# One store for the rows shared by four batches, and a new order of a planned kernel

## The chip, the cores and the metric

The kernel runs on one core of a Trainium2 chip. The metric is the device time of one execution in microseconds; the median of several runs is compared. A core has TensorE (PE, with its weight loads PEld), VectorE (DVE), ScalarE (ACT), GpSimd (POOL) and SyncE (SP), each with its own queue of instructions in order, and 16 DMA engines, which move what SP and ACT issue.

## What is computed

The reference chains three layers, all in 32-bit floats. Attention has 4 batches, 8 heads, 512 local and 32 shared (global) rows of width 64. A local row sees its own neighbourhood of 32 to either side and the shared rows, a shared row sees everything. The output is 4 x 544 = 2,176 rows of 512.

```python
out_g = np.matmul(sm(s_g), v_all)
a_l = sm(np.concatenate([s_lg, np.where(mask, s_ll, -1e9)], axis=-1))
out_l = np.matmul(a_l, np.concatenate([v_g, v_l], axis=2))
```

The second layer is dense: `h = x @ w_in` (512 to 1,024), `h * softmax(h)`, a layer norm, `@ w_out` (back to 512). The third is a soft mixture of 8 experts with 4 slots each: `logits = x @ phi`, a softmax over the rows gathers 32 slot inputs, each expert applies `relu(s @ w1) @ w2`, and a softmax over the slots spreads the 32 results over all rows: `out = c @ slot_out`.

## The kernel before, in words

The work is cut into operations, small groups of instructions of one engine with the buffers that they read and write: 1,571 of them. There are 16 tiles of 128 local rows for attention (`local_tile`) and one of shared rows per batch (`global_tile`); 17 dense tiles of 128 rows (`dense_tile`), of which the last, tile 16, holds the 4 x 32 shared rows; and a tail that needs all rows, since the gathering softmax runs over them: expert layers, and the product `c @ slot_out` with its stores (`tail`).

In the trace PE's lines are these. L743 and L821: scores of local and shared rows. L773, L852, L963: transposes on PE (products with the unit matrix L773 and L963 among them). L788 and L863: weights times v. L900: the dense product, 24 per tile, written as three products of rounded parts. L984: logits. L1050: gathering of slots. L1178 and L1225: the two expert layers. L1259: the last product. L883: transposes into a spare buffer that only keep PE active. ACT has the exponentials (L756, L920), many evictions of accumulators (L775, L968, L1265), DVE the maxima, products and the other evictions (L751, L915, L923, L1267).

The last product is done in two pieces of columns, 320 and 192 (`PIECES`), each behind its own half of L1225. Per piece the 16 local tiles are evicted to SBUF in groups of two (320 columns) or four (192) and stored by SP (L1272): 8 stores of 320 KB and 4 of 384 KB. Tile 16 goes separately: its rows 32b to 32b+31 belong to the first 32 rows of batch b, 544 rows apart in the output. `store` (L1269) issues one transfer of 32 rows per batch (L1274), on SP for the first piece and on ACT's queue for the second.

All of the order comes from a planner in the kernel's own text. `Schedule.run` (L170) plays the operations through on a model of the engines, with a duration for each, a latency between each two engines and a pool of 47 SBUF slots (`NSLOT`) and 8 accumulator banks. At each point an idle engine takes, of its operations that are ready and find a buffer, the one with the least number in the table `PRIORITY` (L403; L1344 overwrites the priority that the builder gave). `CAPS` limits how many slots a class of buffers may hold at once (L229), `KEEP` reserves slots for a class that still needs them (L240). On PE an operation whose array shape differs from the one before is handicapped by `STAY` (L259). The durations are arguments of `op`; those of the stores count SP as occupied for the time of the transfer. The engines then get their instructions in the planned order, and on the chip each runs them in order, waiting on semaphores.

SP also issues all loads in its planned order (L554): q, k and v of the batches, the weights of the dense layer (split into high and low parts by DVE, ACT and POOL, L607 to L618) and the 64 blocks of expert weights. A load waits in SP's queue until its slot is free, and what is behind it waits too.

Of the kernel before, what the change touches and what calls it, by code (L numbers as in the profile page):

```python
# [18 lines left out]
B, H, SL, SG, HD = 4, 8, 512, 32, 64  # L19
DM, DF, NE, SPE = 512, 1024, 8, 4  # L20
NS = NE * SPE
SEQ = SL + SG
# [344 lines left out]
def rank(names, name):  # L367
# [6 lines left out]
CAPS = dict(h=12, p1=61, E=13, W=58, eT=24, lT=5, ln=26, q=34, u=14, v=52, wst=13, xhl=67, xp=16)  # L374
KEEP = dict(p1=3, E=2, W=5, eT=2, eg=21, lT=1, ln=3, mkx=10, u=2, v=2, w=8, wo=28, wst=8, xhl=4, xp=1)
# [13 lines left out]
STAY = 0.448683864814  # L389
# [121 lines left out]
def kernel_body(ctx: ExitStack, tc: tile.TileContext, q, k, v, w_in, w_out, phi, gl, w1, w2, cst, out):  # L511
    nc = tc.nc
    ctx.enter_context(tc.manual_schedule())
    sch = Schedule({"sb": NSLOT, "ps": 8}, CAPS, KEEP, {"k": (3, B)})
    buf, slot, op = sch.buf, sch.slot, sch.op
# [609 lines left out]
    def tail():  # L1125
# [17 lines left out]
        for n, (d0, d1) in enumerate(STEPS):  # L1143
            w = 128 * (d1 - d0)
# [294 lines left out]
```

## Time and profile before

| what | us |
|---|---|
| median of 3 runs | 293.09 |
| the three runs | 291.93, 293.09, 294.32 |
| the profiled execution | 293.87 |
| span of the profiled execution, first to last instruction | 292.1 |

The profile's page is taken from one execution. Its span is shorter than that execution's time by 1.8 us, which lie before the first and behind the last instruction. Busy times of PE are modelled from the issue of the matmuls, since these are pipelined.

### The profile page before, as it was taken

The numbers are of one execution on the slowest core, as the hardware profiler recorded it, in microseconds if no ns is written. First come the engines' busy times: TensorE is split into PE (matmuls) and PEld (weight loads), VectorE is DVE, ScalarE is ACT, GpSimd is POOL, SyncE is SP. The second block draws the span as 40 slices with busy tenths as digits, with TensorE's granted clock in tenths as the row PEclk, the third lists the DMA queues.
The fourth block names the chain that finished last, engine by engine and source line by source line (L and its number), as shares of the span: only waits on it lengthen the run. The fifth ranks groups of instructions, "written<-read, shape, count | busy, mean of one in ns | idle before, by whom it ended". The sixth has DMA issues, their size and how long they took to land.

```text
span 292.1 us, 10948 instructions
## 1 busy us (share of the span) xinstructions
PE 265.6 (91%) x4378; PEld 198.9 (68%) x4378; DVE 202.3 (69%) x752; ACT 196.5 (67%) x650; POOL 100.5 (34%) x171
## 2 busy tenths in 40 slices
PE   0268899999999999999999999999999999999992
PEld 0255578877767787787887887868887775354571
DVE  1789999999855599959987989359849851020351
ACT  2499989975979789998689885547556850220331
POOL 2796874822302346132322335034232431300000
PEclk9999799999999999999999999999999999999999
DMA  7999999926955402364792759997587898999297
GB/s 252 378 402 411 407 404 399 369 85 233 305 207 148 156 14 74 122 242 149 249 301 105 218 166 292 352 360 287 145 287 264 328 331 247 301 332 326 74 344 235
DMA packets 33651, 75.23 MB, mean 258 GB/s; under 512 B 3008, under 2 KB 15936, under 8 KB 33216
## 3 DMA queue, kind: packets, MB, share of 16 engines
q1 hardware_dynamic: 33408, 74.43, 73.1%
q8 instruction: 34, 0.56, 0.8%
q14 instruction: 17, 0.14, 0.1%
q10 hardware_dynamic: 192, 0.10, 0.1%
HBM read 67.83 MB, written 4.46 MB: 247 GB/s over the span
## 4 chain that ended last, share of the span: by engine, by line
PE 81%; DMA 6%; DVE 4%; ACT 3%; issue 2%; SPq 0%; ACTq 0%
PE h L900 32%; PE p L743 6%; PE p L1225 5%; PE p L1178 5%; PE p L773 4%; PE p L788 4%; PE p L963 4%; DMA q<-in_q 3%; PE p L984 3%; PE p L1050 2%; PE p L863 2%; DMA mkx<-in_cst 2%; PE p L1259 2%; PE p L852 2%; PE p L883 1%
## 5 line engine op out<-in xcount | busy, mean ns | idle before, releaser
L900 PE MATMUL h<-w,xhl 128*128 128x512 f32 x408 | 106.8, 405 | 1.5 <-issue 0.7
L900 PEld LDWEIGHTS h<-w,xhl 128*128 128x128 f32 x408 | 72.7, 189 | 18.3 <-issue 2.5
L756 ACT ACTIVATE E<-E,nmx 128x128 f32<-128x128 f32 x128 | 49.7, 394 | 1.0 <-DVE nmx L751 0.7
L743 PE MATMUL p<-k,q 64*32 64x128 f32 x1024 | 21.8, 300 | 16.0 <-DMA q<-in_q 15.1
L751 DVE CUSTOM_DVE_ANT_0 E<-p,mkx 128x128 f32<-128x128 f32 x128 | 29.0, 285 | 4.3 <-PE p L743 4.3
L743 PEld LDWEIGHTS p<-k,q 64*32 64x32 f32 x1024 | 16.5, 115 | 20.9 <-issue 15.4
L920 ACT ACTIVATE u<-h,st 128x512 f32<-128x512 f32 x34 | 23.1, 684 | 8.3 <-DVE st L916 8.0
L892 POOL TENSOR_TENSOR xhl<-xp,xhl 128x512 fp32r<-128x512 f32 x16 | 20.6, 1288 | 14.8 <-ACT xhl L891 14.6
L756 ACT ACTIVATION_READ_ACCUMULATOR E<-E,nmx 128x1 f32 x128 | 24.7, 193 | 0.0
L923 DVE SCALAR_TENSOR_TENSOR u<-h,u 128x512 f32<-128x512 f32 x34 | 22.8, 683 | 2.1 <-ACT u L920 2.0
L915 DVE TENSOR_REDUCE st<-h 128x1 f32<-128x512 f32 x34 | 22.6, 685 | 1.3 <-PE h L900 1.3
L773 PE MATMUL p<-cs,E 128*128 128x128 f32 x128 | 20.4, 293 | 1.9 <-ACT w L630 1.2
L974 POOL TENSOR_TENSOR st<-st,eps 128x1 f32<-128x1 f32 x17 | 10.0, 586 | 31.8 <-DVE st L971 31.8
L775 ACT ACTIVATE eT<-p 128x512 f32<-128x512 f32 x32 | 18.2, 593 | 4.0 <-PE p L773 3.7
L969 ACT ACTIVATE u<-ln 128x1024 f32<-128x1024 f32 x17 | 18.1, 1063 | 3.2 <-DVE ln L942 3.2
L788 PE MATMUL p<-v,eT 128*32 128x64 f32 x1024 | 18.9, 222 | 0.3 <-ACT lT L968 0.2
L773 PEld LDWEIGHTS p<-cs,E 128*128 128x128 f32 x128 | 15.7, 148 | 5.1 <-issue 2.0
L788 PEld LDWEIGHTS p<-v,eT 128*32 128x32 f32 x1024 | 16.2, 111 | 3.3 <-issue 0.9
L795 DVE TENSOR_TENSOR eT<-p,r 128x256 f32<-128x256 f32 x32 | 12.7, 418 | 5.3 <-ACT E L756 1.8
L968 ACT ACTIVATE lT<-p 128x512 f32<-128x512 f32 x25 | 14.2, 595 | 2.6 <-PE p L963 2.5
L963 PE MATMUL p<-cs,ln 128*128 128x128 f32 x104 | 15.2, 277 | 0.4 <-DVE eT L795 0.4
L618 POOL TENSOR_SCALAR W<-W 128x512 f32<-128x512 f32 x8 | 11.9, 1492 | 9.4 <-ACT W L617 9.4
(144 smaller groups left out, 533.2 us busy)
## 6 DMA issues: line engine op xcount, KB each, us to landing
unit<-in_w SPq DMA_DIRECT2D x48, 512.0 KB, 5.6
v<-in_v SPq DMA_DIRECT2D x28, 512.0 KB, 6.9
k<-in_k SPq DMA_DIRECT2D x3, 1536.0 KB, 6.4
wst<-in_w_in SPq DMA_DIRECT2D x8, 512.0 KB, 8.9
wst<-in_w_out SPq DMA_DIRECT2D x8, 512.0 KB, 10.6
k<-in_w SPq DMA_DIRECT2D x8, 512.0 KB, 5.2
q<-in_q SPq DMA_DIRECT2D x6, 512.0 KB, 7.6
out<-unit SPq DMA_DIRECT2D x8, 320.0 KB, 4.8
```

Of the source, the lines that this page charges most:

```text
L743: nc.tensor.matmul(out=sp[hh][32 * c : 32 * c + 32, a2 + i, :], lhsT=Q[rows, 4 * (a2 + i) + c, :], rhs=K[rows, c, s : s + 128], start=True ...
L751: nc.vector.tensor_tensor_reduce(out=E[:, hh, a, :], in0=sp[hh][:, a, :], in1=MK(mask_kind(4 * t + a)), scale=-SCALE, scalar=3.0e38, op0=A ...
L756: nc.scalar.activation(out=E[:, hh, a, :], in_=E[:, hh, a, :], func=AF.Exp, bias=nmx[:, hh, a : a + 1], scale=-1.0, accum_out=sm[:, hh, a ...
L773: nc.tensor.transpose(out=tp[:, a, :], in_=E[:, hh, a, :], identity=I())
L775: op("ACT", 478, lambda hh=hh, tp=tp: nc.scalar.activation(out=eT[hh].ap, in_=tp.ap, func=AF.Copy), (tp,), (eT[hh],))
L788: nc.tensor.matmul(out=av[32 * c : 32 * c + 32, hh, a, :], lhsT=eT[hh][:, a, 32 * c : 32 * c + 32], rhs=V[:, (g - 1) % 2, 64 * h : 64 * h ...
L892: op("Pool", 1250, lambda: nc.gpsimd.tensor_tensor(out=xl.ap, in0=X.ap, in1=xh.ap.bitcast(F32), op=ALU.subtract), (X, xh), (xl,), port=True)
L900: nc.tensor.matmul(out=hp[n].ap, lhsT=lhs[:, kt, :], rhs=rhs[kt][n].ap, start=(kt == 0 and lhs is xh and rhs is whi), stop=(kt == 3 and lh ...
L915: op("DVE", 602, lambda n=n: nc.vector.tensor_reduce(out=part(7 + n), in_=hp[n].ap, axis=AX.X, op=ALU.max, negate=True), (hp[n],), (col[7 ...
L920: op("ACT", 664, lambda n=n: nc.scalar.activation(out=u[:, n, :], in_=hp[n].ap, func=AF.Exp, bias=nm(), scale=1.0, accum_out=part(7 + n)), ...
L923: op("DVE", 613, lambda n=n: nc.vector.scalar_tensor_tensor(out=u[:, n, :], in0=hp[n].ap, scalar=1.0, in1=u[:, n, :], op0=ALU.mult, op1=AL ...
L963: nc.tensor.transpose(out=tp[:, n, :], in_=ln[:, f // 2, 128 * (f % 2) : 128 * (f % 2) + 128], identity=I())
```

## The change

The four transfers of tile 16 per piece become one, whose target takes the first 32 rows of each batch and whose source is the whole tile of 128 rows. The prices of full stores in the planner change, and the limits, the reserves, STAY and all numbers of the table are new. The table has 1,565 numbers in place of 1,571.

```diff
-CAPS = dict(h=12, p1=61, E=13, W=58, eT=24, lT=5, ln=26, q=34, u=14, v=52, wst=13, xhl=67, xp=16)
-KEEP = dict(p1=3, E=2, W=5, eT=2, eg=21, lT=1, ln=3, mkx=10, u=2, v=2, w=8, wo=28, wst=8, xhl=4, xp=1)
+CAPS = dict(h=10, p1=67, E=20, W=52, eT=32, lT=8, ln=35, q=40, u=20, v=53, wst=20, xhl=72, xp=20)
+KEEP = dict(p1=1, E=2, W=2, eT=2, eg=16, lT=1, ln=3, mkx=8, q=1, u=2, v=2, w=6, wo=5, wst=5, xhl=4, xp=1)
...
-STAY = 0.448683864814
+STAY = 1.13106627204
...
-                def store(eng, b=None, j0=j0, ob=ob, cols=cols, group=group):
-                    if b is None:
+                def store(eng, rest=False, j0=j0, ob=ob, cols=cols, group=group):
+                    if not rest:
                         r0 = (j0 // 4) * SEQ + SG + 128 * (j0 % 4)
                         eng.dma_start(out=out[r0 : r0 + 128 * group, cols].rearrange("(k p) d -> p k d", p=128), in_=ob.ap)
                     else:
-                        eng.dma_start(out=out[b * SEQ : b * SEQ + SG, cols], in_=ob[32 * b : 32 * b + 32, 0, :])
+                        eng.dma_start(out=out.rearrange("(b s) d -> b s d", b=B)[:, 0:SG, cols], in_=ob[:, 0, :])
                 if j0 < 16:
-                    op("SP", max((1.45 * w + 25.0) * group, 430), lambda store=store: store(nc.sync), obr, ())
+                    op("SP", max((1.28 * w + 52.0) * group, 430), lambda store=store: store(nc.sync), obr, ())
+                elif ends:
+                    op("ACT", 450, lambda store=store: store(nc.scalar, True), obr, ())
                 else:
-
-                    for b in range(B):
-                        if ends:
-                            op("ACT", 450, lambda store=store, b=b: store(nc.scalar, b), obr, ())
-                        else:
-                            op("SP", 430, lambda store=store, b=b: store(nc.sync, b), obr, ())
+                    op("SP", 430, lambda store=store: store(nc.sync, True), obr, ())
```

The table is left out of the diff: every number differs, and a single one says nothing. What the prediction uses of it are the numbers of the PE operations, sorted by size, and of the first loads.

## Rows read from the trace of the kernel before

**Rows 1.** The page, busy time, share of the span and instructions per engine.

```profile
PE 265.6 (91%) x4378; PEld 198.9 (68%) x4378; DVE 202.3 (69%) x752; ACT 196.5 (67%) x650; POOL 100.5 (34%) x171
```

**Rows 2.** Stages: us, then busy of PE, PEld, DVE, ACT, POOL, clock, DMA share, GB/s.

```profile
17.00:36.00 19.00, 16.20 (x358) 12.28 (x359) 17.45 (x73) 18.00 (x65) 14.93 (x15) 0.91 1.03 407
36.00:273.00 237.00, 233.86 (x3782) 175.37 (x3784) 169.25 (x642) 164.88 (x555) 75.86 (x146) 1.00 0.71 242
273.00:287.00 14.00, 13.57 (x183) 9.73 (x175) 6.43 (x15) 6.03 (x15) 0.00 (x0) 1.00 0.71 240
287.00:292.10 5.10, 0.00 (x0) 0.00 (x0) 0.00 (x0) 0.00 (x0) 0.00 (x0) 0.91 0.69 219
```

**Rows 3.** Waits of PE from 36 to 287: us in total, times, longest.

```profile
PE p L743 <- issue: 0.9, 2, 0.7
...
PE p L963 <- DVE eT L795: 0.4, 1, 0.4
```

**Rows 4.** The page, the chain that ended last, by engine.

```profile
PE 81%; DMA 6%; DVE 4%; ACT 3%; issue 2%; SPq 0%; ACTq 0%
```

**Rows 5.** The chain of waits from 207 to 223: start us, us, what.

```profile
209.33 1.38 PE h L900 x6
210.70 0.57 PE p L984 x16
...
211.71 0.44 PE p L984 x16
212.14 1.59 PE h L900 x6
```

**Rows 6.** PE's timeline, 36 to 287, first and last of 383: start us, us.

```profile
35.80 0.86 PE L900 MATMUL h<-w,xhl 128*128 128x512 f32 x3
...
285.58 0.98 PE L883 MATMUL p<-cs 128*128 128x128 f32 x7
```

**Rows 7.** SP's timeline at the end: stores of shared rows, then full stores.

```profile
274.44 1.76 SPq L1274 DMA_DIRECT2D out<-unit  x4
276.31 11.27 SPq L1272 DMA_DIRECT2D out<-unit  x12
```

**Rows 8.** ACT's timeline, 283.5 to 287.1: evictions, and issues on ACT's queue.

```profile
284.32 0.38 ACTq L1274 DMA_DIRECT2D out<-unit  x1
284.81 0.49 ACT L1265 ACTIVATE unit<-p 128x384 f32<-128x384 f32 x1 [0.52 <-ACT unit L1265]
284.83 0.40 ACTq L1274 DMA_DIRECT2D out<-unit  x1
285.28 0.49 ACT L1265 ACTIVATE unit<-p 128x384 f32<-128x384 f32 x1
285.31 1.16 ACTq L1274 DMA_DIRECT2D out<-unit  x2
286.51 0.49 ACT L1265 ACTIVATE unit<-p 128x384 f32<-128x384 f32 x1 [0.73 <-issue]
```

**Rows 9.** SP's timeline from 287 us: the last store.

```profile
287.02 0.55 SPq L1272 DMA_DIRECT2D out<-unit  x1
```

**Rows 10.** Stages of the end, columns as in rows 2.

```profile
284.50:285.50 1.00, 1.00 (x17) 0.97 (x16) 0.57 (x2) 0.69 (x2) 0.00 (x0) 1.00 0.49 155
285.50:290.50 5.00, 1.07 (x11) 0.75 (x7) 0.79 (x2) 0.76 (x2) 0.00 (x0) 1.00 1.01 319
290.50:292.10 1.60, 0.00 (x0) 0.00 (x0) 0.00 (x0) 0.00 (x0) 0.00 (x0) 0.72 0.02 5
```

**Rows 11.** DMA issues: queue, count, KB each, median us to landing.

```profile
out<-unit SPq DMA_DIRECT2D x4, 384.0 KB, 3.7
...
out<-unit SPq DMA_DIRECT2D x4, 40.0 KB, 1.6
```

**Rows 12.** The v blocks' loads, 60 to 200 us.

```profile
DMA to landing us min/median/max: 3.5/5.5/8.5
```

**Rows 13.** Waits of SP's queue, 60 to 180: us in total, times, longest.

```profile
SPq L554 <- DVE xp L799: 14.8, 3, 11.7
```

**Rows 14.** The chain of waits at 134 us: start us, us, what.

```profile
134.14 3.36 DMA v<-in_v
```

205 rows, old and new, of the table PRIORITY are left out of this document.

## The prediction, made before the changed kernel ran

> **What bounds the kernel now.** I read the busy shares first [rows 1]: PE 91% of the 292.1 us span, DVE and ACT under 70%. That is an average, so the stages come next [rows 2]. Between 36 and 273 us PE is busy 233.86 of 237.00 us at a granted clock of 1.00; before that (17 to 36) 2.8 us of 19 are open, and in the last stage PE does nothing for 5.1 us while the DMA engines are 69% busy. So three different things set the time: the first loads and the splitting of weights up to about 36 us, PE in the long middle, and the stores at the end. The waits of PE in the middle [rows 3] are small, 0.9 and 0.4 us at most in a group. The chain that ended last [rows 4] says the same: 81% of the span is PE itself.
>
> A busy PE is not a PE at its peak. The matrix engine works in three array shapes here: 128*128 (L900, the transposes), 128*32 (L788, L863, L984, L1050, the expert layers) and 64*32 or 64*128 (L743, L821, L1259). In the chain of waits [rows 5] six L900 matmuls take 1.38 us when PE stood in that shape already and 1.59 when it came from L984: 0.21 us for the change into 128*128. Sixteen L984 take 0.44 us in their own shape and 0.57 as the first after L900: 0.13 us. A change costs 0.17 us on average. I went down PE's timeline from 36 to 287 us, 383 merged rows between the two shown [rows 6], and counted 91 changes of shape: 91 x 0.17 = 15.5 us. With the 3.1 us of open time this is what an order can win at all in the middle: the matmuls themselves stay the same.
>
> **The change part by part.**
>
> *Shared rows of piece 1 (320 columns), on SP.* Three of four issues go. They stand from 274.44 to 276.20 (1.76 us for four, 0.44 each [rows 7]), so SP is 1.32 us freer. The next store, at 276.31, follows on the evictions of its two tiles, and the DMA engines have hardly anything to do before it. I take 0; if the stores were bound by SP's issues, it would be -1.3.
>
> *Shared rows of piece 2 (192 columns), on ACT's queue.* The four issues stand between ACT's last evictions [rows 8]; together 1.94 us, so three of them some 1.5. The eviction before the last ends at 285.28 + 0.49 = 285.77, the last starts at 286.51, with two issues between. Without them it starts up to 0.74 us earlier, and the last full store, which SP issues at 287.02 [rows 9], goes with it. But the DMA engines are what ends last: from 285.5 to 290.5 they are 1.01 busy at 319 GB/s, and only 284.5 to 285.5 is half open (0.49) [rows 10]. Four stores of 384 KB and 96 KB of shared rows are 1.67 MB, 5.2 us at 319 GB/s. An earlier last store joins a queue that is already full, so its transfer is hidden. I take -0.1; the lower end is -0.5, the open half of that one microsecond.
>
> On the other side: bytes and rows of the single transfer are those of the four. Where the trace has no transfer whose target steps over batches first, its price lies between none and what it costs if it spreads worse over the 16 engines: 96 KB over all of them is 98,304 B / 319 GB/s = 0.31 us, over a quarter four times that, 1.23, so +0.9 at most. I take none, since every store seen here, 40 KB or 384 KB [rows 11], behaves like its bytes. The Trainium skill says otherwise in "DMA: Bandwidth & Descriptors", section "Why a DMA increments its semaphore by 16 and not by 1": a queue of SP or ACT spreads a transfer over the largest number of engines, up to 16, that divides the slowest dimension of both sides. By that rule four batches on the target side give four engines, where 32 rows gave 16; no row of this trace has such a transfer. It is the rival called "a quarter of the engines" below.
>
> *Store prices.* The planner's 978 ns for a full store of piece 1 becomes 923, the 1,214 ns of piece 2 become 1,191. Nothing of that is on the chip; it acts through the order alone.
>
> *The new order.* The numbers of all 1,565 operations, the class limits, the reserves and STAY change, so every instruction of every engine may move, and with it each load that SP issues in order. No row shows where each of them lands, so I bound the sum. The loads up to q0, the last that the first attention tiles wait for, are the same set in the new table (one v block for another), so the first 17 us stay. In the middle, STAY, the handicap for an operation in another array shape, goes from 0.45 to 1.13. The PE entries sorted by number alone change shape 199 times in the old table and 189 times in the new one; taken in proportion, 91 x 10 / 199 = 4.6 changes fewer, and the larger handicap adds to that. I take 8 fewer: 8 x 0.17 = -1.4 us. Of the 3.1 us open in the middle I take -0.4, since a wait that goes leaves PE with another engine close behind (DVE and ACT are busy 70% of that stage [rows 2]). The lower end is a quarter of the changes and all of the open time: 23 x 0.17 + 3.1 = -7.0. The upper end is a load that comes late: a v block takes 5.5 us at the median and 8.5 at most from issue to landing [rows 12], and if PE has nothing else to do then, that is +5.5.
>
> In the last stage the table puts the product of the shared rows (L1259) behind the other products of its piece, where it had come early. The small transfer is then the last one, and the first full store of piece 2 can start some tenths earlier; I leave this inside the -0.1.
>
> *Sum.* 0 - 0.1 + 0 - 1.4 - 0.4 = -1.9 us. The profiled execution took 293.87 us (span 292.1 and 1.8 around it), 0.8 above the median of 293.09. Its own time becomes 292.0; the same -1.9 from the median is 291.2, which I predict, as runs are compared by their medians.
>
> **The rivals.**
>
> *The order wins more.* For it speaks that 15.5 us go into changes of shape and that STAY more than doubles; against it, that data dependences force many of them (a tile's scores, transposes and products have three shapes). A fifth of the changes (18 x 0.17 = 3.1) and half of the open time (1.5) give -4.6 with the end: 288.5.
>
> *A quarter of the engines.* The middle goes as forecast (-1.8), and the last drain ends 0.9 later, since the DMA engines are full there: -0.9, 292.2.
>
> *A late load: slower.* SP issues in order, and one load that waits for a buffer holds up all behind it: it stood 11.7 us on one such buffer [rows 13], with PE covered by other work, and a v landing already lies on the chain for 3.36 us at 134 [rows 14]. The new limits let more of other classes into the same 47 slots (E 13 to 20, eT 24 to 32) and reserve less (wo 28 to 5). The mechanism is one v block of batches 1 to 3 that lands behind the first L788 or L863 that reads it. From one uncovered landing on it decides: +5.5 - 1.9 = +3.6, 296.7.
>
> *Nothing to see.* The order trades changes of shape for waits: 293.1.
>
> **How the numbers follow.** Forecast 0.42, the order wins more 0.28, a quarter of the engines 0.15, late load 0.10, nothing to see 0.05. About 1% (2.9 us) is what a measurement of this kernel tells from no change. Faster by over 1% is all of the second case and 0.04 of the forecast's lower side: 0.32. Slower by over 1% is the late load: 0.10. The rest is 0.58. The range leaves out the extreme of the second case below and most of the late load above: 287.6 to 295.0; the forecast's own is 289.5 to 292.7.
>
> **What would show it.** Right: counted on PE's timeline, some 83 changes of shape between 36 us and the end of PE, and PE's end near 285; the DMA engines still full from the second piece's first store to about 1.6 us before the end. The ACT queue has one issue of about 0.4 us, and ACT's last two evictions follow on each other without the 0.74 us between them, while the end moves less than that. Wrong: 91 or more changes with a shorter span (then it was waits); a wait of PE for v over 2 us (late load); a drain in which the mean DMA share falls to about a quarter after the last full store while a shared store is still under way (a quarter of the engines).

## The result and the profile after

| | median us | lowest to highest | runs |
|---|---|---|---|
| before | 292.99 | 291.93 to 297.63 | 20 |
| after | 295.36 | 293.47 to 296.90 | 20 |

The changed kernel is slower: the ratio is 1.0066 with a 95% interval from 1.0047 to 1.0085, some 1.9 us of 293. That is clear of no change and under 1%. (The two medians alone would give 1.0081.) I had forecast 291.2 and a range up to 295.0; the median lies 0.4 us above it.

The profiled execution of after took 295.09 us, its span is 293.3. That of before took 293.87, 0.9 above its median of 20 runs, that of after 0.3 below its own. So the two spans differ by 1.2 us where the medians differ by 2.4: about half of what the change cost doesn't show between the two traces, and the places must be confirmed by runs.

The page's busy shares and chain, and the stages, which answer to [rows 1, 2, 4]:

```profile
PE 265.0 (90%) x4378; PEld 199.0 (68%) x4378; DVE 202.6 (69%) x752; ACT 196.1 (67%) x650; POOL 102.1 (35%) x171
...
PE 80%; DVE 6%; DMA 5%; ACT 4%; issue 2%; SPq 0%; DVEq 0%; ACTq 0%
```

```profile
17.00:36.00 19.00, 16.20 (x401) 12.56 (x386) 17.70 (x73) 17.79 (x65) 14.50 (x14) 1.00 1.03 406
36.00:273.00 237.00, 233.24 (x3742) 174.91 (x3745) 168.71 (x639) 164.09 (x554) 77.38 (x146) 1.00 0.70 242
273.00:287.00 14.00, 13.05 (x171) 9.48 (x161) 6.52 (x15) 5.97 (x15) 0.00 (x0) 1.00 0.71 238
287.00:293.30 6.30, 0.00 (x0) 0.00 (x0) 0.00 (x0) 0.00 (x0) 0.00 (x0) 0.57 0.60 182
```

The long middle is nearly the same: PE is busy 233.24 us of 237 where it was 233.86. Counted on PE's timeline in the same way, it changes its array shape 90 times from 36 us to its end, 91 times before. What has grown is the last stage, where PE does nothing: 6.3 us for 5.1.

SP's timeline at the end, which answers to [rows 7, 9] (start us, us, what; x8 and x4 are merged rows):

```profile
274.67 6.32 SPq L1271 DMA_DIRECT2D out<-unit  x8
282.25 0.71 SPq L1273 DMA_DIRECT2D out<-unit  x1
283.07 4.46 SPq L1271 DMA_DIRECT2D out<-unit  x4
```

The first full store of piece 2 in the kernel before:

```profile
284.24 0.37 SPq L1272 DMA_DIRECT2D out<-unit  x1
```

All eight full stores of piece 1 go first now, and the single transfer of its shared rows stands right in front of the four full stores of piece 2. The first of these is issued at 283.07, 1.2 us earlier than before. From there to the end it was 7.9 us (284.24 to 292.1) and is 10.2 (283.07 to 293.3). The stages show where these go, against [rows 10] (last two columns: DMA share, GB/s):

```profile
283.00:284.00 1.00, 1.00 (x15) 0.78 (x13) 0.76 (x2) 0.80 (x2) 0.00 (x0) 1.00 0.27 72
284.00:285.00 1.00, 1.00 (x13) 0.90 (x13) 0.69 (x2) 0.61 (x3) 0.00 (x0) 1.00 0.35 80
285.00:285.50 0.50, 0.50 (x7) 0.50 (x6) 0.14 (x1) 0.24 (x2) 0.00 (x0) 1.00 0.79 238
285.50:290.50 5.00, 0.57 (x6) 0.33 (x4) 0.00 (x0) 0.00 (x0) 0.00 (x0) 0.74 0.98 303
290.50:291.00 0.50, 0.00 (x0) 0.00 (x0) 0.00 (x0) 0.00 (x0) 0.00 (x0) 0.50 0.41 135
291.00:291.50 0.50, 0.00 (x0) 0.00 (x0) 0.00 (x0) 0.00 (x0) 0.00 (x0) 0.50 0.23 77
291.50:292.00 0.50, 0.00 (x0) 0.00 (x0) 0.00 (x0) 0.00 (x0) 0.00 (x0) 0.50 0.11 37
```

Two stretches are new. From 283 to 285 the 16 DMA engines have a mean share of a quarter to a third, although a full store was issued at 283.07. And behind the drain, where the share fell from full to nothing in one step [rows 10], it now runs out over 1.5 us at 0.41, 0.23 and 0.11: a few engines still write while the others are done. What they write can be told by queue (packets, MB, share), first from 288 to 290.5 us, then from 290.5 to 292:

```profile
q1 hardware_dynamic: 790, 0.59, 81.5%
q10 hardware_dynamic: 132, 0.10, 13.1%
...
q1 hardware_dynamic: 176, 0.12, 24.7%
```

q1 is SP's queue, q10 is ACT's, which carries the shared rows of piece 2 alone. All of these rows are written by 290.5 us. What runs out behind them are full stores, on as many engines as a share of about a quarter has room for.

How many engines the single transfer uses can be read from the packets of ACT's queue over the whole execution (the page's DMA queues: packets, MB, share), before and after:

```profile
q10 hardware_dynamic: 192, 0.10, 0.1%
...
q10 hardware_dynamic: 132, 0.10, 0.1%
```

Before it was 192 packets: four transfers of 32 rows, 128 in all, and 64 more, 16 for each transfer. Now it is 128 rows and 4 more. SP's queue, with the shared rows of piece 1, lost the same 60 (33,408 to 33,348). The rule of the Trainium skill that the prediction gave as a rival ("DMA: Bandwidth & Descriptors", section "Why a DMA increments its semaphore by 16 and not by 1") says that each engine that takes part ends with one write of its own to the semaphore; by its rule on the slowest dimension a target stepping over four batches first goes on 4 engines. The trace agrees: 64 = 4 x 16 before, 4 = 1 x 4 after.

### The profile page after: what moved, and what is told of

Read it like the earlier page. It is cut to its first block, busy times and chain, and to the rows that moved or that the text cites. A ratio compares the mean times of both kernels' runs of the same rounds, so it can differ in the third digit from the quotient of the medians.

```text
span 293.3 us, 10933 instructions
## 1 busy us (share of the span) xinstructions
PE 265.0 (90%) x4378; PEld 199.0 (68%) x4378; DVE 202.6 (69%) x752; ACT 196.1 (67%) x650; POOL 102.1 (35%) x171
## 3 DMA queue, kind: packets, MB, share of 16 engines
q1 hardware_dynamic: 33348, 74.43, 72.0%
## 4 chain that ended last, share of the span: by engine, by line
PE 80%; DVE 6%; DMA 5%; ACT 4%; issue 2%; SPq 0%; DVEq 0%; ACTq 0%
PE h L899 30%; PE p L1224 5%; PE p L787 5%; PE p L742 5%; PE p L1177 5%; PE p L772 4%; PE p L962 4%; DMA q<-in_q 3%; PE p L983 3%; PE p L1049 3%; PE p L882 2%; PE p L862 2%; PE p L1258 2%; PE p L851 2%; DMA mkx<-in_cst 2%
## 5 line engine op out<-in xcount | busy, mean ns | idle before, releaser
L742 PE MATMUL p<-k,q 64*32 64x128 f32 x1024 | 21.2, 291 | 16.8 <-DMA k<-in_k 12.0
L742 PEld LDWEIGHTS p<-k,q 64*32 64x32 f32 x1024 | 15.9, 112 | 21.0 <-issue 15.8
L973 POOL TENSOR_TENSOR st<-st,eps 128x1 f32<-128x1 f32 x17 | 10.8, 635 | 25.9 <-DVE st L970 25.7
L926 POOL TENSOR_SCALAR st<-st 128x1 f32<-128x1 f32 x17 | 5.2, 307 | 34.2 <-ACT u L919 26.7
```

Of the source, the lines that this page charges most:

```text
L742: nc.tensor.matmul(out=sp[hh][32 * c : 32 * c + 32, a2 + i, :], lhsT=Q[rows, 4 * (a2 + i) + c, :], rhs=K[rows, c, s : s + 128], start=True ...
```

## The experiments

Theory 1, "quarter": the single transfer runs on 4 of 16 engines, is long by itself and holds up the stores behind it. Theory 2, "order": the transfers are as good as before, and the new order of the last stage costs. The first four runs cross the two orders with the forms of the transfer. All ratios are to the kernel before, with 95% intervals.

**The new order with four transfers.**

```diff
-                        eng.dma_start(out=out.rearrange("(b s) d -> b s d", b=B)[:, 0:SG, cols], in_=ob[:, 0, :])
+                        for b in range(B):
+                            eng.dma_start(out=out[b * SEQ : b * SEQ + SG, cols], in_=ob[32 * b : 32 * b + 32, 0, :])
```

> The changed kernel with its plan, but each single transfer issued as the four of before. Quarter theory (the single transfer runs on 4 of 16 engines and holds up what is behind it): the low DMA shares of 283 to 285 us and after 290.5 us go. The four issues on SP (1.76 us in place of 0.71) put the first full store of piece 2 at about 284.0 in place of 283.07, and from there to the end it is 7.9 us as before: span 291.9, ratio to before 0.999 (0.997 to 1.001). Order theory (the new order of the last stage is what costs): span stays at 293.3 or grows by the longer issues, ratio 1.006 or more.

Measured: 293.85 us, 1.0039 (1.0017 to 1.0061), span 292.1. It lies between the ranges of the two theories and meets neither: better than the changed kernel, not as good as the kernel before. SP's timeline and the stages say why.

```profile
282.14 1.75 SPq L1274 DMA_DIRECT2D out<-unit  x4
283.99 2.95 SPq L1271 DMA_DIRECT2D out<-unit  x4
```

```profile
282.50:285.00 2.50, 2.50 (x31) 2.18 (x32) 1.75 (x4) 1.62 (x5) 0.00 (x0) 1.00 0.47 142
285.00:290.00 5.00, 0.96 (x9) 0.72 (x7) 0.02 (x1) 0.13 (x1) 0.00 (x0) 0.95 1.00 315
290.00:290.50 0.50, 0.00 (x0) 0.00 (x0) 0.00 (x0) 0.00 (x0) 0.00 (x0) 0.50 0.59 162
```

The run-out is gone, as the quarter theory says. The gap ahead of the drain stays (0.47), and its cause is now another: four issues of 0.44 us stand in front of the first full store, in an order that was made for one. They put the first full store at 283.99; from there to the end it is 8.1 us, close to the 7.9 of the kernel before.

**The old order with the single transfer.**

```diff
-                        eng.dma_start(out=out[b * SEQ : b * SEQ + SG, cols], in_=ob[32 * b : 32 * b + 32, 0, :])
+                        if b == 0:
+                            eng.dma_start(out=out.rearrange("(b s) d -> b s d", b=B)[:, 0:SG, cols], in_=ob[:, 0, :])
```

> The kernel before with its plan, but the shared rows stored in one transfer per piece (the other three issues left out). Quarter theory: ACT's queue shows about 132 packets in place of 192, and the last drain ends 0.9 us later or more (four engines have 24.6 KB more to write in place of 6.1): span 293.0 to 294.5, ratio 1.003 to 1.008. Order theory: the transfer itself costs nothing and three issues on ACT go: span 291.6 to 292.1, ratio 0.998 to 1.000.

Measured: 294.74 us, 1.0070 (1.0042 to 1.0099). This one edit costs all that the whole change costs, without any new order. ACT's queue has 132 packets, as expected. Its last drain:

```profile
284.50:287.00 2.50, 1.69 (x21) 1.35 (x19) 1.02 (x2) 0.98 (x2) 0.00 (x0) 1.00 0.90 293
287.00:289.00 2.00, 0.00 (x0) 0.00 (x0) 0.00 (x0) 0.00 (x0) 0.00 (x0) 0.80 0.89 214
289.00:290.50 1.50, 0.00 (x0) 0.00 (x0) 0.00 (x0) 0.00 (x0) 0.00 (x0) 0.50 0.91 312
290.50:292.00 1.50, 0.00 (x0) 0.00 (x0) 0.00 (x0) 0.00 (x0) 0.00 (x0) 0.50 0.18 61
```

From 287 to 289 the engines are busy at 0.89 and move 214 GB/s in place of some 319: 2.0 x (1 - 214/319) = 0.7 us lost. The run-out takes 1.5 us and moves in it, at 61 GB/s, what full engines move in 0.3, so 1.2 is lost. Together that is 1.9 us beside the 2.1 of the ratio. The match is rough: the span of this execution is only 1.2 us longer than that of the kernel before.

**One transfer on 16 engines, new order and old order.** Row 4s+b of the last tile holds shared row s of batch b, so the target's slowest step counts 32; the permuting eviction takes 0.40 us in place of 0.27. The second run has the same edit in the kernel before, with three of the four issues left out.

```diff
-                op("ACT", 158, lambda cp=cp, ct=ct: nc.scalar.activation(out=ct[0:64], in_=cp[0:64, 0:1, :], func=AF.Copy), cpr, (ct,))
+                op("ACT", 158, lambda cp=cp, ct=ct: nc.scalar.activation(out=ct[0:64, 0, :].rearrange("p (s b) -> p b s", b=B),
+                    in_=cp[0:64, 0, :].rearrange("p (b s) -> p b s", b=B), func=AF.Copy), cpr, (ct,))
...
-                        eng.dma_start(out=out.rearrange("(b s) d -> b s d", b=B)[:, 0:SG, cols], in_=ob[:, 0, :])
+                        eng.dma_start(out=out.rearrange("(b s) d -> s b d", b=B)[0:SG, :, cols], in_=ob[:, 0, :])
```

> The changed kernel with its plan and still one transfer per piece, but row 4s+b of the tile holds shared row s of batch b (the eviction of the combine weights permutes its columns), so that the target's slowest step has 32 entries. Quarter theory: the transfer takes 16 engines, its issue is about 0.4 us, the first full store of piece 2 is issued at 283.1 and the end comes 7.9 us later: span 291.0, ratio to before 0.996 (0.994 to 0.998). Theory that one transfer with rows far apart is slow by itself, or order theory: 293.3, ratio 1.006.

> The kernel before with its plan, one transfer per piece in the form that steps over 32 rows first. Quarter theory: nothing is held up, three issues go from SP and three from ACT; the last drain was full, so the end moves by 0 to -0.5 us: span 291.6 to 292.1, ratio 0.998 to 1.000. Theory that one transfer is slow by itself: as the kernel before with one transfer, 293 or more.

Measured: 1.0008 (0.9982 to 1.0033) in the new order, 0.9980 (0.9956 to 1.0004) in the old one. The second is as expected, the first misses its 0.994 to 0.998. One transfer is not slow by itself; the order of its steps is what made it slow. In the new order that alone takes the ratio from 1.0066 to 1.0008, 1.7 us, in the old one from 1.0070 to 0.9980, 2.6 us. The new order with the spread transfer: the queue's packets (128 rows and 16), SP's issues, and the stages.

```profile
q10 hardware_dynamic: 144, 0.10, 0.1%
```

```profile
281.84 0.63 SPq L1273 DMA_DIRECT2D out<-unit  x1
282.57 3.27 SPq L1271 DMA_DIRECT2D out<-unit  x4
```

```profile
282.50:283.50 1.00, 1.00 (x17) 0.78 (x13) 0.67 (x2) 0.71 (x2) 0.00 (x0) 1.00 0.60 206
283.50:288.50 5.00, 2.15 (x21) 1.81 (x21) 0.91 (x2) 0.94 (x3) 0.00 (x0) 1.00 0.98 319
288.50:289.00 0.50, 0.00 (x0) 0.00 (x0) 0.00 (x0) 0.00 (x0) 0.00 (x0) 0.89 0.85 281
289.00:289.50 0.50, 0.00 (x0) 0.00 (x0) 0.00 (x0) 0.00 (x0) 0.00 (x0) 0.50 0.04 14
```

With nearly the same order of stores as in the changed kernel, the drain is full 0.9 us behind the first full store (282.57 to 283.50) and ends in one step. In the changed kernel it was full some 2.2 us behind it.

**Half of the change.** The quarter transfer in one piece, four transfers in the other, in the new order.

```diff
-                        eng.dma_start(out=out.rearrange("(b s) d -> b s d", b=B)[:, 0:SG, cols], in_=ob[:, 0, :])
+                        if eng is nc.sync:
+                            for b in range(B):
+                                eng.dma_start(out=out[b * SEQ : b * SEQ + SG, cols], in_=ob[32 * b : 32 * b + 32, 0, :])
+                        else:
+                            eng.dma_start(out=out.rearrange("(b s) d -> b s d", b=B)[:, 0:SG, cols], in_=ob[:, 0, :])
```

The second run has `nc.scalar` in the place of `nc.sync`.

> The changed kernel; the shared rows of piece 1 as four transfers on SP, those of piece 2 as one on 4 engines. Theory that the loss sits in the last drain (piece 2): the tail of low DMA share after 290 us stays, ratio to before 1.006 (1.004 to 1.008), as the changed kernel. Theory that it sits in front of piece 2's stores (piece 1): the quarter share around 283 to 285 us goes, ratio 1.003 to 1.004.

> The changed kernel; the shared rows of piece 1 as one transfer on 4 engines, those of piece 2 as four on ACT's queue. Theory that the loss sits in the last drain: the DMA share falls from full to nothing within 0.5 us at the end, and the ratio to before is that with four in both pieces, 1.003 to 1.005. Theory that it sits in front of piece 2's stores: 1.006 or more.

Measured: 1.0067 (1.0037 to 1.0097) with four in piece 1, 1.0057 (1.0032 to 1.0082) with four in piece 2. The first is as its theory says, the second misses its 1.003 to 1.005, and intervals of 0.3% to either side can't part the two. The ratio with four in piece 1 doesn't price the quarter transfer of piece 2 alone either, since the four issues again leave a gap ahead of the drain (a share of 0.47 from 283 to 285, as in the first run). The stages still show the two costs one by one: with four in piece 1 the run-out stays (the first view), with four in piece 2 it goes, while the quarter transfer ahead of the drain stays (the second).

```profile
290.00:292.00 2.00, 0.00 (x0) 0.00 (x0) 0.00 (x0) 0.00 (x0) 0.00 (x0) 0.50 0.18 61
```

```profile
283.00:285.00 2.00, 2.00 (x24) 1.68 (x21) 1.58 (x3) 1.61 (x4) 0.00 (x0) 1.00 0.34 77
285.00:290.00 5.00, 0.83 (x8) 0.59 (x6) 0.00 (x0) 0.01 (x1) 0.00 (x0) 0.91 1.02 326
290.00:290.50 0.50, 0.00 (x0) 0.00 (x0) 0.00 (x0) 0.00 (x0) 0.00 (x0) 0.50 0.52 154
```

**The quarter transfer of piece 1 on the other queue.** Is the gap ahead of the drain a hold-up of the queue, or only four busy engines?

```diff
-                    op("SP", 430, lambda store=store: store(nc.sync, True), obr, ())
+                    op("SP", 430, lambda store=store: store(nc.scalar, True), obr, ())
```

> The changed kernel; its single transfer of piece 1 on 4 engines is issued on ACT's queue in place of SP's, at the same place of the order. Hold-up theory (a transfer on 4 engines stops the stores behind it in the same queue, on the other 12 engines too): SP's first full store of piece 2 is issued as before or earlier and the DMA share rises to 0.9 within 1.2 us of that issue, not 2.1 us as in the changed kernel; ratio to before 1.002 to 1.005. Sharing theory (the four engines are merely longer busy): the share between stays at a quarter to a third for as long as in the changed kernel, ratio 1.006.

Measured: 296.46 us, 1.0119 (1.0090 to 1.0149). The ratios that I expected are missed by far, under either theory. SP issues the first full store of piece 2 at 281.97, and the engines are full 1.0 us later:

```profile
282.00:283.00 1.00, 1.00 (x17) 0.78 (x13) 0.67 (x2) 0.49 (x1) 0.00 (x0) 1.00 0.38 134
283.00:284.50 1.50, 1.03 (x10) 0.76 (x11) 0.91 (x2) 0.87 (x2) 0.00 (x0) 1.00 1.00 308
284.50:286.50 2.00, 1.42 (x12) 1.18 (x11) 0.00 (x0) 0.33 (x1) 0.00 (x0) 1.00 0.87 181
286.50:289.00 2.50, 0.00 (x0) 0.00 (x0) 0.00 (x0) 0.00 (x0) 0.00 (x0) 0.95 0.96 295
289.50:291.50 2.00, 0.00 (x0) 0.00 (x0) 0.00 (x0) 0.00 (x0) 0.00 (x0) 0.50 0.25 80
```

This is a weaker test than I had planned. ACT issues the small transfer at 282.36, behind an eviction, and its first row is written at 284.1, when the full store already has all engines. So the run shows the full store with no small transfer in front of it, and doesn't part the two theories. It does show the cost of sharing: the small transfer's bytes now go into the last drain, and at the end there is a quarter share for 2.0 us, in which both queues still write. That fits the same four engines for both pieces; the trace doesn't name the engines.

What happens behind the quarter transfer can be read from the changed kernel's own trace, record by record, since a row of piece 1 is 1,280 bytes long and one of piece 2 768. From 283.6 to 285.8 some four rows of 1,280 bytes are under way at a time, as four engines would have it. The full store issued at 283.07 writes its first row 1.3 us later, where it was 0.9 in the kernel before. Then it has one to four rows under way up to 285.0 and some twelve only from 285.4, while the small transfer still runs; in the kernel before it was at twelve 0.2 us behind its first row. So sharing alone doesn't explain the gap, since the other engines had nothing else to do, and a full stop until the small transfer ends doesn't either: the full store starts late and slowly behind it. What slows it is not shown.

**The two orders again, transfers alike.** The two kernels with one transfer on 16 engines once more, side by side on the same chip.

> The changed kernel with the spread transfer once more, beside the kernel before with the same transfer on the same chip, to set the new order against the old one with the transfers alike. Theory that the new order gains nothing: the two ratios differ by under 0.3%, this one 0.998 to 1.002. Theory of the prediction (order -1.8 us): this one is 0.6% under the other, 0.992 to 0.995.

> The kernel before with the spread transfer once more. Its last drain was full, so 0.996 to 1.000 of the kernel before by either theory.

Measured: 293.05 us, 0.9998 (0.9975 to 1.0022) in the new order; 292.83 us, 0.9983 (0.9957 to 1.0009) in the old one. They differ by 0.15%, the first pair by 0.28% in the same direction, both within the intervals. PE's line of the first expert layer (first and last start us) stands within 0.3 us of the same place in both (the counts differ because some of its weights lie in another buffer); the new order first, then the old one:

```profile
L1177 PE MATMUL p<-unit,lps x112: 592/592/617, 243.9 to 257.2; 128*32 128x512 f32 x112
```

```profile
L1178 PE MATMUL p<-unit,lps x116: 592/592/617, 243.6 to 257.0; 128*32 128x512 f32 x116
```

The spans are 290.5 and 290.4. So the new order gains nothing, and it costs nothing that can be told from none here; the 0.6% of the forecast is ruled out.

**What a change of shape costs.** STAY alone was set to other values at which the planner finds a plan. The plans' own counts, 101 and 99 in the expectations, include what comes before 36 us, where the timeline's 91 and 90 begin.

```diff
-STAY = 0.448683864814
+STAY = 0.95
```

The second run has 0.6 in place of 1.131 in the new order with the spread transfer.

> The kernel before with STAY at 0.95 in place of 0.449 and all else the same: its plan then has 115 changes of PE's array shape in place of 101. By the prediction's price of 0.17 us a change, 14 more cost 2.4 us: ratio to before 1.008. Theory that a change is mostly covered (weight loads and matmuls of the next shape start beside the last of the old): under 0.5 us, ratio 1.000 to 1.002, as far as the plan brings no wait of its own on PE.

> The changed kernel with the spread transfer and STAY at 0.6 in place of 1.131: its plan has 128 changes of shape in place of 99. By 0.17 us a change 29 more cost 4.9 us: ratio to before 1.017 (against 1.001 for the same with 99). Theory that a change is mostly covered: 1.001 to 1.004.

Measured: 325.61 us, 1.1087 (1.1032 to 1.1141), and 329.86 us, 1.1239 (1.1179 to 1.1298). Both theories are missed by some thirty us. PE's waits in the first of them, all over the span:

```profile
PE p L963 <- DVE st L933: 3.9, 1, 3.9
PE p L1015 <- ACT lps L1012: 3.6, 4, 1.2
PE p L997 <- ACT eg L835: 3.0, 1, 3.0
```

These are waits that the kernel before doesn't have; they are part of the loss, and where the rest lies was not followed up. So the runs say nothing on the price of a change of shape. They say that the table and STAY belong together: with another handicap the same numbers give a plan a tenth slower.

## Why the prediction was wrong

*Shared rows of piece 1, taken at 0.* The 0 held, as far as seen, for transfers on 16 engines in the old order, where these issues stand ahead of any full store. It didn't hold for the quarter transfer even there: with it the engines are full some 1.6 us behind the issue of the first full store (275.47), with the spread transfer 1.0 (275.18). And the new order puts the transfer right in front of the first full store of piece 2. I had read from the table that the shared rows' product comes last, and had called it a gain of some tenths; I didn't follow it into SP's queue. There it delays the drain by more than 1 us (2.2 us from issue to full engines, against 0.9 with the spread transfer).

*Shared rows of piece 2, -0.1 from a drain that was full anyway.* Not contradicted, as far as the issues go: with the spread transfer in the old order the two runs give 0.9980 and 0.9983, some -0.5 us, the lower end of that step, with intervals that include 1. These runs leave out three issues on each queue, so they don't part piece 2 from piece 1. The changed kernel has one issue on ACT's queue, of 1.15 us where I had written about 0.4; ACT's last two evictions follow on each other as forecast, and the end didn't follow them.

*The unknown spread of the single transfer, taken at 0, at most +0.9.* This is the first of the two steps that failed. I took the value of the nearest rows, although those were all transfers over 128 or 32 rows, and gave the quarter 0.15. It came true, and even the bound was too small: the runs show 1.7 us in the new order (1.0066 against 1.0008) and 2.6 in the old one (1.0070 against 0.9980). The bound counted the 96 KB of piece 2 alone; the 160 KB of piece 1, by the same sum 0.51 us on all engines and 2.05 on a quarter, were left out. And it took the transfer as the last thing to end. In the traces the full stores end last. With the single transfer in the old order they run out late, which costs some 1.2 us, and while both queues write another 0.7 is lost.

*The new order, -1.8.* This is the second step that failed: no such gain came. 8 changes of shape fewer were taken, one fewer came (90 for 91 on the timeline); of 3.1 us open in the middle 0.4 was to go, and 3.8 are open now. Sorting the table by its numbers said little of the order that came of it; the planner also goes by readiness and buffers. The 0.17 us per change remain read from the chain; no run tests them. With the transfers alike the two orders differ by 0.15 to 0.28%, the new one behind. The two failed steps add up: from the forecast's -1.9 us to the measured +1.9 it is 3.8, of which the transfer on four engines is 1.7, and the rest, with the spread transfer at +0.2 in place of -1.9, is mostly the gain that the order didn't bring.

*The rivals.* "A quarter of the engines" had the right mechanism; its 292.2 was still a gain, since it kept the order's -1.8, and its price was too small. There was no late load: PE's longest waits from 36 us on have no releaser in a transfer, as before.

```profile
PE p L742 <- issue: 2.2, 3, 1.7
```

*What was to show it* did in part: the share falls to about a quarter at the end. But no shared store is still under way then, as the packets by queue show; it is the full stores that are late.

## What to carry to other kernels

Fewer transfers are not cheaper if the one that is left spreads worse: count the slowest step of both sides of a transfer. Here 4 entries went on a quarter of the engines and 32 on all of them, for the same 128 rows. Look at the packets of a queue against the rows moved, and at a DMA share that runs out at a quarter. Moving a transfer that spreads badly is no cure: in front of the large ones it delayed them, and inside their drain it cost more (1.0119). Spreading it was the cure.

## What the runs showed that I had not expected

A transfer on four engines delays the stores behind it in its queue on the other engines as well. In the changed kernel the mean share stayed at about a quarter until 284.5 us, though a 384 KB store had been issued at 283.07; behind the spread transfer the engines were full 0.9 us after that store's issue. And a quarter of the engines doesn't always move a quarter of the full rate. A quarter of the 319 GB/s of the full drain is 80, and the run-outs at a quarter share have 77 to 80; but in the gap of the changed kernel two half microseconds have 54 and 53 (last column). A row of 1,280 bytes takes 0.105 us there on average and 0.059 from 284.5 to 285.9, when these rows alone come to 91 GB/s; why the first rows are slow is not shown.

```profile
283.50:284.00 0.50, 0.50 (x7) 0.33 (x5) 0.50 (x2) 0.50 (x2) 0.00 (x0) 1.00 0.29 54
284.00:284.50 0.50, 0.50 (x10) 0.50 (x9) 0.26 (x1) 0.14 (x1) 0.00 (x0) 1.00 0.26 53
```

The old order with one spread transfer is clearly faster than the changed kernel (0.9980 and 0.9983 against 1.0066); its gain of 0.2% over the kernel before is not parted from none.
